# Splitting one group's projection by real and imaginary half instead of by chunk, with the neighbour's half visit moved between the two

## The chip, the cores and the metric

The kernel runs on one core of a Trainium2 chip. The metric is the device time of one execution in microseconds (us). A profiled execution has a "span" as well, from its first to its last recorded instruction; it is some 2 us shorter than the metric. All runs quoted here were timed on the same chip as runs of the kernel before. Times "at" some microsecond are counted from the start of the span.

## The reference, cut to what matters

The output is `x + S5(xn) + MoE(xn)`, where `xn` is the layer norm of `x` (2048 tokens of 1024).

```python
# state-space layer (S5), 1024 complex states
Lam_bar = exp(dt * Lam)
B_bar   = ((Lam_bar - 1) / Lam)[:, None] * (B_re + 1j * B_im)
Bu      = einsum("bld,pd->blp", xn + 0j, B_bar)        # projection into the states
h[t]    = Lam_bar * h[t-1] + Bu[t]                     # recurrence over 2048 tokens
y       = 2 * einsum("blp,dp->bld", h, C).real + xn * Dskip
# mixture of experts: the two tokens with the largest r = xn @ w_r get an MLP on top
...
```

The complex projection is two real ones, with `B_re` and with `B_im`. The change touches only the order in which parts of it are computed at the very start.

## The kernel before

Tokens go in 8 frames of 256 (two chunks of 128 each), states in 8 groups of 128. For a frame `f` and a group `j`, TensorE computes the real and the imaginary half of the projection into one PSUM tile; one such piece of work is called a visit. ScalarE evicts the tile (`evac_u`), VectorE rotates, scans and rotates back, and TensorE multiplies by C.

```python
def stage_Bu(f, j, ts_=slice(0, TF)):              # TF = 256 tokens, T = 128
    if (f, j) not in pB_tiles:
        pB_tiles[f, j] = psum.tile([128, 2, TF], F32, name="pB", tag="B", bufs=3)
    pB = pB_tiles[f, j]
    for ri in range(2):                            # real, imaginary
        for k in range(DT):                        # 8 blocks of the inner dimension
            nc.tensor.matmul(out=pB[:, ri, ts_], lhsT=BT[ri][j][:, k, :], rhs=xnT_tiles[f][:, k, ts_],
                             start=(k == 0), stop=(k == DT - 1))

def evac_u(f, j):
    ...
    nc.scalar.copy(out=u_tiles[f][:, :, j, :], in_=pB_tiles.pop((f, j))[:])

HALVES = ((0, 0), (0, 1), (1, 0), (1, 1), (1, 2))  # these are visited one chunk at a time
```

For the pairs in `HALVES` there are two visits, `("Bh", f, j)` on the first chunk and `("Bu", f, j)` on the second, so that TensorE has work before the second chunk is normalized. Each of them needs the real *and* the imaginary weights of its group. The weights come by transposed loads, real ones first.

The order on every engine is not written down. Each piece of work is a task with a modelled duration, dependencies and a key; a small list scheduler plays the program through and emits the tasks in the order that comes out. `ADJUST` holds hundreds of fitted offsets to the keys.

```python
add(("Bh", f, j), "PE", 0.93, ..., [("B", j, 0), ("B", j, 1), ("xnT", f * CPF)] + ..., key=2 * f - 3 + j / 8, ...)
...
pl.run().emit()
```

## Time and profile before

| | before |
|---|---|
| time, median of the 3 runs made before the prediction (range) | 266.6 us (266.29 to 266.65) |
| span of the profiled execution | 264.4 us |
| TensorE / VectorE / ScalarE busy | 97% / 95% / 60% |
| TensorE's stall for group 1's imaginary weights | 1.13 us, ending at 13.1 |
| VectorE's wait that follows from it | 0.30 us, to 17.48 |

How to read it: two engines are nearly full and feed each other for the whole span. A stall on one is worth something at the end only if the other moves with it, and if nothing takes it back in the next 250 us. The lines behind the last two rows stand in the prediction below.

### The profile page before, as it was taken

To read this page: it belongs to the slowest core of one execution; us is meant where nothing else is said; L and a number is where in the kernel's file an instruction comes from. 1 tells how busy PE (TensorE), PEld (TensorE's weight loads), DVE (VectorE), ACT (ScalarE), POOL (GpSimd) and SP (SyncE) were. 2 spreads that over 40 slices of the span, in tenths; PEclk is the share of its full clock that TensorE was granted. 3 is DMA by queue.
4 is the path that set the end of the run, shared out by engine and by line. 5 is a ranking of instruction groups with operands and counts; after the bars stand their busy time and mean duration, and the time that the engine had idled before them with its cause. 6 is when DMAs were issued, how large, how long until landed. Compare 5 with 4: busy or idle time off the path is not lost.

```text
span 264.4 us, 5522 instructions
## 1 busy us (share of the span) xinstructions
PE 256.5 (97%) x2207; PEld 173.2 (66%) x2227; DVE 251.5 (95%) x334; ACT 158.9 (60%) x281; POOL 83.6 (32%) x126
## 2 busy tenths in 40 slices
PE   7799999999999999999999999999999999999994
PEld 7799988774688457456756586455864776644461
DVE  6999999999999999999999999999998999999992
ACT  3799999959699999996524447034551533145110
POOL 4221303563545440731040217115260409011100
PEclk9999999999999999999999999999999999999999
DMA  8999999998541125416111197588967884770411
GB/s 180 188 175 218 171 235 229 248 271 293 153 137 57 47 60 165 138 40 183 58 62 60 35 360 237 187 266 287 296 235 253 289 272 175 269 288 20 117 46 40
DMA packets 66165, 46.51 MB, mean 176 GB/s; under 512 B 45844, under 2 KB 52122, under 8 KB 66140
## 3 DMA queue, kind: packets, MB, share of 16 engines
q1 hardware_dynamic: 65788, 45.82, 63.4%
q8 instruction: 17, 0.28, 0.5%
q0 software_dynamic: 144, 0.27, 0.3%
q10 hardware_dynamic: 208, 0.07, 0.1%
q14 instruction: 8, 0.07, 0.1%
HBM read 30.94 MB, written 4.20 MB: 133 GB/s over the span
## 4 chain that ended last, share of the span: by engine, by line
PE 61%; DVE 28%; issue 3%; SPq 2%; ACT 2%; DMA 2%; DVEq 0%
PE pB L646 34%; PE pY L849 20%; DVE gf L718 9%; DVE ot L863 3%; PE pG L1048 3%; DVE hT L759 3%; DVE m L760 3%; DVE v L699 2%; DVE v L697 2%; DVE m L698 2%; DMA BT<-in_A_B_im_dram 2%; DVE gb L711 2%; SPq L286 2%; PE pD L1088 1%; PE pY L842 1%
## 5 line engine op out<-in xcount | busy, mean ns | idle before, releaser
L646 PE MATMUL pB<-xnT,BT 128*128 128x256 bf16 (+1 forms) x1104 | 117.5, 265 | 1.1 <-DMA BT<-in_A_B_im_dram 1.1
L849 PE MATMUL pY<-CT,hT 128*128 128x512 bf16 (+1 forms) x508 | 114.8, 372 | 1.7 <-issue 0.5
L646 PEld LDWEIGHTS <-BT 128*128 128x128 bf16 x1104 | 99.7, 98 | 16.2 <-issue 3.2
L849 PEld LDWEIGHTS <-hT 128*128 128x128 bf16 x528 | 49.1, 98 | 52.6 <-issue 3.2
L734 POOL TENSOR_TENSOR cw<-gf,tL 128x16 f32<-128x16 f32 (+1 forms) x38 | 35.0, 924 | 136.1 <-DVE gf L718 135.2
L718 DVE TENSOR_TENSOR_SCAN gf<-R,v 128x1040 f32<-128x1040 f32 (+1 forms) x38 | 69.0, 1851 | 0.2
L652 ACT CAST u<-pB 128x512 bf16<-128x512 f32 x64 | 36.5, 580 | 34.8 <-PE pB L646 34.7
L724 ACT CAST gb<-gf 128x1024 bf16<-128x1024 f32 (+1 forms) x38 | 32.4, 862 | 24.6 <-DVE gf L718 24.5
L810 ACT ACTIVATE xa<-xr,nmr_all,rstd_all 128x1024 f32<-128x1024 bf16 x12 | 14.9, 1239 | 21.9 <-DMA xr<-in_A_x_dram 8.1
L699 DVE TENSOR_TENSOR v<-v,m 128x2048 bf16<-128x2048 bf16 (+2 forms) x22 | 20.6, 938 | 0.8
L761 DVE TENSOR_TENSOR hT<-hT,m 128x2048 bf16<-128x2048 bf16 (+2 forms) x22 | 20.5, 934 | 0.8
L759 DVE TENSOR_TENSOR hT<-gb,E2c 128x2048 bf16<-128x2048 bf16 (+2 forms) x22 | 20.5, 930 | 0.2
L697 DVE TENSOR_TENSOR v<-u,E1c 128x2048 bf16<-128x2048 bf16 (+2 forms) x22 | 20.4, 928 | 0.2
L760 DVE TENSOR_TENSOR m<-gb,E2s 128x2048 bf16<-128x2048 bf16 (+2 forms) x22 | 20.5, 930 | 0.0
L698 DVE TENSOR_TENSOR m<-u,E1s 128x2048 bf16<-128x2048 bf16 (+2 forms) x22 | 20.4, 930 | 0.0
L863 DVE TENSOR_TENSOR ot<-pY,xa 128x512 bf16<-128x512 f32 (+1 forms) x25 | 16.0, 656 | 2.4 <-PE pY L852 1.8
L749 POOL CAST v<-cy 128x16 bf16<-128x16 f32 (+1 forms) x19 | 14.1, 744 | 1.4
L349 ACT ACTIVATE xn<-xt,nmean_all 128x1024 bf16<-128x1024 bf16 x12 | 13.8, 1149 | 0.3
L742 POOL TENSOR_TENSOR cy<-cw 128x16 f32<-128x16 f32 (+1 forms) x19 | 12.8, 674 | 1.5
L343 ACT ACTIVATE xn<-xt 128x1024 bf16<-128x1024 bf16 x12 | 12.6, 1054 | 0.0
L374 ACT ACTIVATE xn<-xt,nmr_all,rstd_all 128x1024 bf16<-128x1024 bf16 x10 | 12.4, 1241 | 0.3
L750 POOL TENSOR_TENSOR v<-cy,v 128x16 bf16<-128x16 f32 (+1 forms) x19 | 11.1, 586 | 1.5
(153 smaller groups left out, 186.6 us busy)
## 6 DMA issues: line engine op xcount, KB each, us to landing
wt<-in_B_w_up_dram SPq DMA_DIRECT2D x14, 512.0 KB, 5.1
wt<-in_B_w_gate_dram SPq DMA_DIRECT2D x14, 512.0 KB, 3.8
wt<-in_B_w_down_dram SPq DMA_DIRECT2D x14, 512.0 KB, 3.9
xt<-in_A_x_dram SPq DMA_DIRECT2D x16, 256.0 KB, 3.1
xr<-in_A_x_dram SPq DMA_DIRECT2D x16, 256.0 KB, 2.5
out_dram<-ot SPq DMA_DIRECT2D x31, 128.0 KB, 2.6
Drow<-in_A_Dskip_dram SPq DMA_DIRECT2D x1, 256.0 KB
xnT<-xn SPq DMA_TRANSPOSE x10, 2.8
```

The costliest lines, as they stand in the source:

```text
L646: nc.tensor.matmul(out=pB[:, ri, ts_], lhsT=BT[ri][j][:, k, :], rhs=xnT_tiles[f][:, k, ts_], start=(k == 0), stop=(k == DT - 1))
L652: nc.scalar.copy(out=u_tiles[f][:, :, j, :], in_=pB_tiles.pop((f, j))[:])
L697: nc.vector.tensor_tensor(out=rot, in0=u, in1=both(E1c, js), op=ALU.mult)
L698: nc.vector.tensor_tensor(out=m[:, :, js, :], in0=u[:, ::-1], in1=E1s[:, :, js, :], op=ALU.mult)
L699: nc.vector.tensor_add(out=rot, in0=rot, in1=m[:, :, js, :])
L718: nc.vector.tensor_tensor_scan(out=flat(gf), data0=flat(R[:, js, :]), data1=flat(v[:, ri, js, :]), initial=0.0, op0=ALU.mult, op1=ALU.add)
L724: nc.scalar.copy(out=gb_tiles[c][:, ri, js, :], in_=gf_tiles[c, js.start, ri][:, :, 2:])
L734: nc.gpsimd.tensor_tensor(out=cw_tiles[c, js.start][:, ri, :, 0:n], in0=g.unsqueeze(1).to_broadcast([128, 2, n]), in1=tL[:, ri, :, js], op ...
L759: nc.vector.tensor_tensor(out=rot, in0=g, in1=E2c[:, :, js, :], op=ALU.mult)
L760: nc.vector.tensor_tensor(out=m[:, :, js, :], in0=g[:, ::-1], in1=both(E2s, js), op=ALU.mult)
L849: nc.tensor.matmul(out=pY[:], lhsT=h_tiles[c][:, ri, j, :], rhs=CT[ri][h][:, j, d0:d0 + w], start=first and c in SKIP_DVE and ri == rs[0] ...
L863: nc.vector.tensor_add(out=y_tiles["ot", c][:, d_], in0=y_tiles.pop(("pY", c, dh))[:], in1=y_tiles["xa", c][:, d_])
```

## The change

Its intent: the first visit of group 1 shall need only the real weights, so that TensorE doesn't stand still until the imaginary ones land. Group 1 of frame 0 is split by half (real over 256 tokens, then imaginary over 256 tokens) in place of by chunk. The first visit of frame 1's group 0 gets an offset of -4.0, which brings it between the two. Cut to its core:

```diff
@@ ADJUST
+    ('Bh', 1, 0): -4.0,
@@
-    def stage_Bu(f, j, ts_=slice(0, TF)):
+    def stage_Bu(f, j, ts_=slice(0, TF), ris=(0, 1)):
...
-        for ri in range(2):
+        for ri in ris:
...
+    RISPLIT = ((0, 1),)
...
-  add(("Bh", f, j), ..., lambda f=f, j=j: stage_Bu(f, j, slice(0, T)), ...
+  add(("Bh", f, j), ..., lambda f=f, j=j: stage_Bu(f, j, ris=(0,)) if (f, j) in RISPLIT else stage_Bu(f, j, slice(0, T)), ...
-  add(("Bu", f, j), ..., lambda ...: stage_Bu(f, j, slice(T if hs else 0, TF)),
+  add(("Bu", f, j), ..., lambda ...: stage_Bu(f, j, ris=(1,)) if (f, j) in RISPLIT else stage_Bu(f, j, slice(T if hs else 0, TF)),
```

On TensorE the four runs of 8 matmuls of 128 columns become two runs of 8 of 256, with frame 1's visit between them.

More of the change, by code (lines that the diff above doesn't have):

```diff
@@ L662 @@
             if hs:
-                add(("Bh", f, j), "PE", 0.93, lambda f=f, j=j: stage_Bu(f, j, slice(0, T)), [("B", j, 0), ("B", j, 1), ("xnT", f * CPF)] + ([] if f else [("xnT0",)]),
+                add(("Bh", f, j), "PE", 0.93, lambda f=f, j=j: stage_Bu(f, j, ris=(0,)) if (f, j) in RISPLIT else stage_Bu(f, j, slice(0, T)), [("B", j, 0), ("B", j, 1), ("xnT", f * CPF)] + ([] if f else [("xnT0",)]),
                     key=2 * f - 3 + j / 8, takes=[("pB", (f, j), [("u", f, j)])])
-            add(("Bu", f, j), "PE", 0.93 if hs else 1.75, lambda f=f, j=j, hs=hs: stage_Bu(f, j, slice(T if hs else 0, TF)),
+            add(("Bu", f, j), "PE", 0.93 if hs else 1.75, lambda f=f, j=j, hs=hs: stage_Bu(f, j, ris=(1,)) if (f, j) in RISPLIT else stage_Bu(f, j, slice(T if hs else 0, TF)),
                 [("B", j, 0), ("B", j, 1)] + [("xnT", f * CPF + cc) for cc in range(CPF)] + ([("Bu", f, j - 1)] if j else [])
```

## The prediction

> **What bounds the kernel now.** I read the page first, then the chain of waits, then the timeline of each engine around the changed stage, then the list of waits of TensorE and VectorE for the whole span.
>
> ```profile
> span 264.4 us, 5522 instructions
> PE 256.5 (97%) x2207; PEld 173.2 (66%) x2227; DVE 251.5 (95%) x334; ACT 158.9 (60%) x281; POOL 83.6 (32%) x126
> ```
>
> Two engines, not one, are nearly full: TensorE 97%, VectorE 95%. A microsecond taken from one of them is worth nothing where the other sets the pace. The chain of waits (start, length, what) begins like this:
>
> ```profile
> 7.65 5.42 DMA BT<-in_A_B_im_dram
> 13.08 0.05 issue
> 13.12 0.62 PE pB L646 x8
> 13.74 0.18 PE r_ps L425 x8
> 13.92 1.81 PE pB L646 x32
> ```
>
> It comes from the transposed load of the imaginary weights of group 1, goes along TensorE to about 56 us, along VectorE from 66 to 119, along TensorE to about 230, and ends on VectorE and TensorE. The load that starts it is the one that this change is aimed at. TensorE's timeline there (start, length, engine, line, operation, tiles, count, idle time before with its releaser):
>
> ```profile
> 9.46 1.05 PE L646 MATMUL pB<-xnT,BT 128*128 128x128 bf16 x16
> 10.35 0.39 PE L430 MATMUL warm<-ident 128*128 128x128 bf16 x4
> 10.93 0.62 PE L403 MATMUL pT<-ident,xn 128*128 128x128 bf16 x8 [0.19 <-DVE xn L363]
> 11.38 0.61 PE L646 MATMUL pB<-xnT,BT 128*128 128x128 bf16 x8
> 13.12 0.62 PE L646 MATMUL pB<-xnT,BT 128*128 128x128 bf16 x8 [1.13 <-DMA BT<-in_A_B_im_dram]
> 13.58 0.34 PE L425 MATMUL r_ps<-wr_cm,xnT 128*128 128x1 bf16 x8
> 13.78 1.95 PE L646 MATMUL pB<-xnT,BT 128*128 128x128 bf16 x32
> 15.57 0.61 PE L403 MATMUL pT<-ident,xn 128*128 128x128 bf16 x8
> ```
>
> At 11.38 the real half of the first chunk of group 1 runs; then TensorE stands still for 1.13 us until the imaginary weights land at 13.08. The 32 matmuls from 13.78 are the second chunk of group 1, then the first visit of frame 1's group 0. It is TensorE's only wait over 0.2 us between 1.4 and 258 us.
>
> ScalarE and VectorE in the same stage:
>
> ```profile
> 14.87 0.58 ACT L652 CAST u<-pB 128x512 bf16<-128x512 f32 x1 [0.55 <-PE pB L646]
> 15.36 1.06 ACT L343 ACTIVATE xn<-xt 128x1024 bf16<-128x1024 bf16 x1
> 16.41 1.05 ACT L545 ACTIVATE sf<-th 128x1024 f32<-128x1024 f32 x1
> 17.48 0.69 DVE L615 CAST E1s<-sf 128x1024 bf16<-128x1024 f32 x1 [0.30 <-ACT sf L545]
> ```
>
> This is how TensorE's stall reaches VectorE: the eviction of group 1 waits 0.55 us, the statistics pass and the sine table queue behind it, and VectorE waits 0.30 us for the sine table. After that VectorE's list of waits has nothing until after 119 us.
>
> **What the Trainium skill says.** "TensorE: Matmul & The Clock Gate", section "Wait — 56ns, not 53.3ns?", gives a warm start-to-start of N / 2.4 GHz plus about 2.5 ns: 55.6 ns for 128 columns, so 109 ns for 256. The trace agrees: (10.35 - 9.46) / 16 = 55.6 ns; and 32 matmuls of 256 columns from 30.07 to the next instruction at 33.57 make 109 ns. The same page's section "Back-to-back issue gap" gives some 81 ns for a weight load with a 128-column matmul in a real kernel; the trace does not agree here, since each of those 16 has its own weight load. This decides whether wider matmuls save time: by the trace hardly any.
>
> "DMA: Bandwidth & Descriptors", section "Anatomy of one DMA — SWDGE (gpsimd) path", puts most of a transfer's fixed cost of about 2 us into the write receipt before its semaphore. Here the issue of the load ended at 9.00 (7.65 + 1.35) and it landed at 13.08, 4.1 us later[...]. The kernel can only work around it, which is what the change does.
>
> The TensorE page's section on the 16 sub-arrays says that ScalarE and VectorE take their queues strictly in order. The three ScalarE lines above agree: the sine table's input is ready before the sine starts, and it starts when the instruction ahead of it ends.
>
> **The change part by part.**
>
> 1. *Matmuls of group 1.* Removed: 4 runs of 8 at 128 columns, 32 x 55.6 ns = 1.78 us. Added: 2 runs of 8 at 256 columns, 16 x 109 ns = 1.75 us. Saving 0.03 us; 16 weight loads fewer, all of them beside matmuls.
>
> 2. *The wait.* The first visit now needs only the real weights, which were there at 11.38, and the second chunk's input, evicted before 9.2. It runs 11.38 to 12.25. Next come the eight 128x1 matmuls and frame 1's moved half visit, both on chunk 2's input; its eviction on ScalarE starts at 11.58 and takes 1.01 us, so it ends at 12.59. Then: 128x1 matmuls 12.64 to 12.84 (0.20, as from 13.58 to 13.78), half visit 16 x 55.6 = 0.89 to 13.73, imaginary visit of group 1 (landed at 13.08, no wait) 0.87 to 14.60. Before, the same work ended at 15.57. TensorE's lead: 0.97 us, made of 1.13 of stall and 0.03 less 0.39 of a new, shorter wait for the eviction, with rounding and hand-overs.
>
> 3. *What that lead is worth.* It is consumed by VectorE:
>
> ```profile
> 36.81 0.54 DVE L358 TENSOR_SCALAR xn<-xt,nmean_all,rstd_all 128x1024 bf16<-128x1024 bf16 x1
> 37.41 0.62 PE L403 MATMUL pT<-ident,xn 128*128 128x128 bf16 x8
> 119.14 0.38 PE L842 MATMUL pY<-dgD,xnT 128*128 128x128 bf16 x4 [0.16 <-DVE ot L863]
> ```
>
> At 37.41 TensorE transposes a normalized chunk that VectorE finished at 37.35: slack 0.06 us. A lead of 0.97 us becomes a wait there unless VectorE is earlier too. The same holds for the first additions into the output at 66.05 (a PSUM ring of three) and at 119.14, where TensorE already waits for VectorE. VectorE has no wait between 17.48 and 119, so it moves only by what the change takes off its 0.30 us.
>
> 4. *VectorE's 0.30 us.* In the same ScalarE order, the eviction of group 1 can start after the imaginary visit ends, 14.60 plus 0.2 of pipeline tail: 14.80 against 14.87, and VectorE gains about 0.07. The half visit was put before the imaginary one, so the group is complete hardly sooner. But instructions are ordered by a list scheduler in the kernel, which thinks the two visits alike in length; there group 1's completion moves one half visit (0.93 in its units) later. ScalarE may then take the statistics pass first, which fits into the 0.55 us of waiting: pass from 14.35, eviction to about 15.95, sine from 15.95 in place of 16.41, and the whole 0.30 goes. I give the first order one chance in three, the second two in three: about 0.2 us.
>
> Sum: 266.6 - 0.2 to 0.3, so 266.3 us.
>
> **The rivals.**
> - *The whole lead arrives*: 266.6 - 1.0 = 265.6. For it: the wait stands on the chain. Against it: the 0.06 us of slack at 37.41 and a VectorE without waits for 100 us.
> - *The next weights become the wait.* TensorE comes to groups 2 to 7 a microsecond sooner. The imaginary load of group 2 was issued at 12.53, that of group 1 took 5.4 us; by that, 17.9, and it would be wanted at 17.1 in place of 18.0. Against it: the earlier transfers queued behind others. It costs only lead that VectorE takes anyway, so 266.5 or so.
> - *The scheduler shuffles later work.* All orders after this point come out of the same simulation; a different tie can move an eviction or an addition by one instruction on VectorE or TensorE (0.7 to 2 us each). The order was tuned for the kernel before, so it is rather worse than better: 266 to 268. For it: hundreds of fitted offsets. Against it: the three visits together take the scheduler's TensorE the same time.
> - *Wider matmuls save weight loads*, as the 81 ns would have it: 32 x 81 against 16 x 109 is 0.85 us. The measured 55.6 ns speaks against it, and item 3 would swallow it.
>
> **Range and chances.** Runs of the kernel before spread over 0.36 us. Between the whole lead with a little more (265.3) and a mild shuffle (267.2) lie most cases. 2% is 5.3 us, five times the stall; only a badly shuffled order could reach it.
>
> **What would show it.** In the changed profile: 8 matmuls of 256 columns at about 11.4 with no wait on the imaginary weights after them; a short wait near 12.6 for the eviction of chunk 2; the 32 matmuls of the stage done near 14.6; the sine table at 16.3 or at 15.9, and VectorE's 0.30 gone in the second case; new TensorE waits on VectorE, 0.6 to 0.9 us in sum, at the transposes near 29 and 37 or near 66. I am wrong if the end moves by over 0.6 us, if TensorE shows no new waits on VectorE, or if VectorE's order differs after 20 us.

## More of the kernel before

The residual input of each chunk is loaded a second time, into a tile with one buffer, and ScalarE consumes it:

```python
xrp = ctx.enter_context(tc.tile_pool(name="xrp", bufs=1))
...
def load_xr(c):
    xr = xrp.tile([128, D], BF16, name="xr")
    nc.sync.dma_start(out=xr[:], in_=x2[c * 128:(c + 1) * 128, :])
```

And `keep_clock` gives TensorE dummy matmuls during the first microseconds, tasks `("warm", i)`.

## The result, and the profile after

| | before | after |
|---|---|---|
| median of 6 runs | 266.59 us | 266.67 us |
| range | 265.90 to 266.65 | 266.38 to 267.21 |
| ratio after / before, 95% interval | | 1.0011 (0.9995 to 1.0027) |

All outputs are right.

The head of the page of the changed kernel:

```profile
span 264.7 us, 5510 instructions
PE 256.9 (97%) x2211; PEld 172.2 (65%) x2211; DVE 251.3 (95%) x334; ACT 159.0 (60%) x281; POOL 83.6 (32%) x126
```

The 16 weight loads are gone (2227 to 2211). Matmuls seem to have grown from 2207 to 2211, but in the trace of before some matmul records are missing. Nothing else has moved, and the span is 0.3 us longer, not shorter. So did the early stage fail to gain? TensorE's timeline there:

```profile
12.16 1.05 PE L647 MATMUL pB<-xnT,BT 128*128 128x256 bf16 x8 [0.54 <-DMA BT<-in_A_B_re_dram]
13.05 0.34 PE L426 MATMUL r_ps<-wr_cm,xnT 128*128 128x1 bf16 x8
13.25 1.93 PE L647 MATMUL pB<-xnT,BT 128*128 128x128 bf16 x24
15.01 0.61 PE L404 MATMUL pT<-ident,xn 128*128 128x128 bf16 x8
```

The wait for the imaginary weights is gone. In its place the real weights came late in this execution: they landed at 12.12, where they had landed at 10.51 before, and cost 0.54 us. Even so the transposes after the stage start at 15.01 in place of 15.57. ScalarE and VectorE:

```profile
14.41 1.06 ACT L344 ACTIVATE xn<-xt 128x1024 bf16<-128x1024 bf16 x1
...
15.47 0.57 ACT L653 CAST u<-pB 128x512 bf16<-128x512 f32 x1
15.96 1.06 ACT L546 ACTIVATE sf<-th 128x1024 f32<-128x1024 f32 x1
...
17.18 0.69 DVE L616 CAST E1s<-sf 128x1024 bf16<-128x1024 f32 x1
```

The statistics pass now fills the time in which ScalarE used to wait 0.55 us for the eviction's input. The sine table starts at 15.96 in place of 16.41, and VectorE's wait of 0.30 us before the cast of that table is gone: 17.18 in place of 17.48. By 20 us VectorE is 0.4 us ahead of the kernel before, and it keeps this lead within 0.02 us until 107 us. So the change does deliver a gain; it is lost later.

Where it is lost is seen when the timelines of the two kernels are laid side by side around 107 us. First the kernel before, one or two rows each from the timelines of SyncE (which issues transfers; start, length of the issue), ScalarE, TensorE and VectorE:

```profile
101.69 1.66 SPq L867 DMA_DIRECT2D out_dram<-ot  x1
103.87 0.34 SPq L805 DMA_DIRECT2D xr<-in_A_x_dram  x1
...
107.10 1.24 ACT L810 ACTIVATE xa<-xr,nmr_all,rstd_all 128x1024 f32<-128x1024 bf16 x1
...
113.20 1.91 PE L646 MATMUL pB<-xnT,BT 128*128 128x256 bf16 x16
...
119.78 1.23 DVE L759 TENSOR_TENSOR hT<-gb,E2c 128x2048 bf16<-128x2048 bf16 x1
```

The same rows of the changed kernel:

```profile
101.29 0.36 SPq L869 DMA_DIRECT2D out_dram<-ot  x1
102.70 0.34 SPq L807 DMA_DIRECT2D xr<-in_A_x_dram  x1
...
107.76 1.24 ACT L812 ACTIVATE xa<-xr,nmr_all,rstd_all 128x1024 f32<-128x1024 bf16 x1 [1.00 <-DMA xr<-in_A_x_dram]
...
113.86 1.91 PE L647 MATMUL pB<-xnT,BT 128*128 128x256 bf16 x16 [0.97 <-ACT u L653]
...
120.44 1.23 DVE L761 TENSOR_TENSOR hT<-gb,E2c 128x2048 bf16<-128x2048 bf16 x1 [1.10 <-ACT gb L726]
```

Read the brackets from top to bottom. ScalarE waits 1.00 us for `xr`, the second load of the residual input. The eviction that follows it in ScalarE's order comes later by that much, so TensorE waits 0.97 us; the copy `gb` of the scan comes later too, so VectorE waits 1.10 us. Before the wait, the changed kernel was 0.4 us ahead, and after it, it is 0.66 us behind (107.76 against 107.10, 113.86 against 113.20, 120.44 against 119.78). VectorE then skips a wait of 0.44 us that the kernel before had at 125 us (0.32 us regained), and the remaining 0.34 us stay to the end.

The strange part is in the first two rows: `xr` was issued 1.17 us *earlier* than before (102.70 against 103.87), and landed later, at 107.68 against 107.02. The transfer's completion comes in 16 parts. Fifteen of them were there at 105.78; the last came 1.9 us after. What ran beside it? The view of the DMA queues shows packets of the kind "instruction", and queue 8 carries large ones. Its row for the stretch 100.5 to 103.5 us of the kernel before (packets, MB, share of 16 engines), and its row for 103.5 to 106.5 us of the changed one; each kernel has no such packet in the other stretch:

```profile
q8 instruction: 1, 0.02, 3.4%
```

```profile
q8 instruction: 1, 0.02, 2.7%
```

Over the whole span this queue has 17 packets and 0.28 MB in both kernels, 16 KB each. The Trainium skill, page "Runtime: NRT & Kernel Launch", section "Instruction fetch mechanics", says that an engine's instructions are refilled in blocks of 16 KiB, 256 instructions, over a DMA queue of the sequencer's own, and that this is mostly hidden. The count fits TensorE alone: its 2211 matmuls and 2211 weight loads make 4422 / 256 = 17.3, and on the page no other engine has more than 334 instructions. That queue 8 is TensorE's is inferred from this; the trace doesn't name its owner. A share of 2.7% of 16 engines for 3 us is 0.027 x 16 x 3 = 1.3 us of one DMA engine. In the kernel before, this fetch started at 101.57, while SyncE was issuing the output store (whose issue took 1.66 us in place of 0.36), and so it was over before `xr` was issued. In the changed kernel it started at 104.79, in the middle of `xr`'s transfer, and ended at 106.06.

What `xr`'s last part did after that can be read from the packets. The load is 256 KB in 16 parts, so 16 KB or 8 packets of 2 KB each. One line of the DMA view of the changed kernel, for 106.04 to 107.20 us:

```profile
DMA packets 218, 0.07 MB, mean 61 GB/s; under 512 B 209, under 2 KB 210, under 8 KB 218
```

Exactly 8 packets of 2 KB or more are left, one part's worth. In the packed trace they run one after another from 106.05 to 107.19: they start when the fetch ends. In the kernel before, `xr` already had nothing to spare: it landed at 107.02 and was used at 107.10, and these 0.08 us are the hand-over, which takes 0.08 to 0.09 us in every trace here in which ScalarE waits for `xr`.

This gives the theory: **32 fewer instructions on TensorE move its instruction fetches, one of them now falls into a transfer that has no slack, and this takes back the gain.** Rivals: the lead itself makes the wait (everything comes 0.4 us earlier, `xr`'s issue among it); the new order on TensorE makes it; chance does.

### The profile page after: what moved, and what is told of

The parts are those of the page before. It is cut to its first block, busy times and chain, and to the rows that moved or that the text cites. A ratio compares the mean times of both kernels' runs of the same rounds, so it can differ in the third digit from the quotient of the medians.

```text
span 264.7 us, 5510 instructions
## 1 busy us (share of the span) xinstructions
PE 256.9 (97%) x2211; PEld 172.2 (65%) x2211; DVE 251.3 (95%) x334; ACT 159.0 (60%) x281; POOL 83.6 (32%) x126
## 4 chain that ended last, share of the span: by engine, by line
PE 62%; DVE 18%; ACT 11%; DMA 5%; issue 3%; SPq 0%; ACTq 0%
PE pY L851 29%; PE pB L647 26%; DVE gf L720 3%; PE pG L1050 3%; DMA wt<-in_B_w_down_dram 2%; ACT xn L350 2%; DMA xr<-in_A_x_dram 2%; ACT xa L812 2%; ACT xn L344 2%; DVE st L335 2%; ACT xn L375 1%; ACT gb L726 1%; PE pY L844 1%; PE pD L1090 1%; DVE ot L865 1%
## 5 line engine op out<-in xcount | busy, mean ns | idle before, releaser
L851 PE MATMUL pY<-CT,hT 128*128 128x512 bf16 (+1 forms) x528 | 118.3, 373 | 0.0
L751 POOL CAST v<-cy 128x16 bf16<-128x16 f32 (+1 forms) x19 | 14.1, 744 | 1.4
```

Of the source, the lines that this page charges most:

```text
L851: nc.tensor.matmul(out=pY[:], lhsT=h_tiles[c][:, ri, j, :], rhs=CT[ri][h][:, j, d0:d0 + w], start=first and c in SKIP_DVE and ri == rs[0] ...
```

## The experiments

Ten runs were made, of nine kernels (`e0_after` is the changed kernel, `e10_swap_again` repeats `e4_swap_only`). Two ideas were given up. With a second buffer for `xr`, 14.1 KB per partition are left for the pool of the expert weights, which needs 16 KB. A dependency that forces the eviction ahead of the statistics pass deadlocked the list scheduler, so in the kernels below two tasks are exchanged after scheduling instead.

### The changed kernel again: `e0_after`

No edit; it tells chance from cause.

> The changed kernel once more, as the comparison for the others. Theory (instruction fetch): VectorE is 0.3 to 0.4 us ahead of the kernel before from 17 to 107 us, then ScalarE waits about 1 us for the load of xr at about 107, since a 16 KB instruction fetch of TensorE at 104 to 105 us holds one DMA engine; time 266.5 to 266.8, ratio to before 1.000 to 1.002. Rival (chance): the wait at 107 was an accident of the one profiled run and is not there again; then 266.2.

Measured: 266.53 us (265.77 to 267.51), ratio 0.9997 (0.9973 to 1.0022). The wait came again; the fetch started at 104.77, and `xr`'s last part came 2.3 us after its fifteenth:

```profile
107.84 1.25 ACT L812 ACTIVATE xa<-xr,nmr_all,rstd_all 128x1024 f32<-128x1024 bf16 x1 [1.11 <-DMA xr<-in_A_x_dram]
```

In this execution the real weights were in time, so it is the better one to test the early steps of the prediction. Three rows of TensorE's timeline, and one of its list of waits (total, times, longest):

```profile
11.42 1.04 PE L647 MATMUL pB<-xnT,BT 128*128 128x256 bf16 x8
12.69 0.35 PE L426 MATMUL r_ps<-wr_cm,xnT 128*128 128x1 bf16 x8 [0.23 <-ACT xnT L416]
...
14.67 0.61 PE L404 MATMUL pT<-ident,xn 128*128 128x128 bf16 x8
```

```profile
PE pT L404 <- DVE xn L359: 0.4, 1, 0.4
```

The visit starts at 11.42 without a wait, a short wait for the eviction of chunk 2 follows, and the stage ends 0.90 us earlier than before. At the transpose near 37 us TensorE then waits 0.4 us for VectorE. VectorE's own lead at 100 us is 0.45 us, half of TensorE's.

### The same order with the instructions put back: `e1_halves`

```diff
         for ri in ris:
-            for k in range(DT):
-                nc.tensor.matmul(out=pB[:, ri, ts_], ..., rhs=xnT_tiles[f][:, k, ts_], ...)
+            for t_ in ((slice(0, T), slice(T, TF)) if len(ris) == 1 else (ts_,)):
+                for k in range(DT):
+                    nc.tensor.matmul(out=pB[:, ri, t_], ..., rhs=xnT_tiles[f][:, k, t_], ...)
```

Order and intent are those of the change; only the two visits of group 1 are cut into 128 columns again, so TensorE has as many instructions as before.

> The changed kernel with each of the two visits by real and imaginary half run as two runs of 128 columns, so that TensorE has as many instructions as before (the change took 32 out) and its 16 KB instruction fetches fall where they fell before; the order of work on every engine is that of the changed kernel. Theory (instruction fetch): the fetch near 104.8 us goes back to about 101, no wait of ScalarE for xr at 107, VectorE's lead of 0.3 to 0.4 us reaches the end: span 264.0, time 266.2, ratio to before 0.9985. Rival (TensorE's lead itself shifts the transfers against each other): the wait at 107 stays, time as the changed kernel's. Rival (width): 32 narrow matmuls cost more than 16 wide ones, by under 0.05 us, not to be seen.

Measured: 266.36 us (265.76 to 267.21), ratio 0.9991 (0.9971 to 1.0011). The fetch is back at 101.38, and of the wait 0.23 us are left:

```profile
107.10 1.24 ACT L813 ACTIVATE xa<-xr,nmr_all,rstd_all 128x1024 f32<-128x1024 bf16 x1 [0.23 <-DMA xr<-in_A_x_dram]
```

VectorE was 0.31 us ahead at 100 us and still 0.32 us at 250 us, and the span is 264.0. The rival "new order on TensorE" falls with this. The small remaining wait comes of the lead and of the fetch's length together: the fetch lasted 1.67 us, `xr` was issued only after it, at 103.95, and landed at 107.02 as in the kernel before, and ScalarE wanted it 0.3 us sooner. The lead alone does not make even this wait, as the next run has a larger lead and none.

### Only the half visit moved: `e3_move_only`

The kernel before plus the one line in `ADJUST`; no split.

> The kernel before with the half visit of frame 1's group 0 moved, without the split into real and imaginary. TensorE keeps its stall of about 1.1 us on the imaginary weights; ScalarE takes the statistics pass first, as in the changed kernel. The group's eviction can start at about 15.8 in place of 14.9, so the sine table comes at 16.3 in place of 16.4: VectorE gains 0.1 us. Instruction fetches as before. Theory: span 264.3, time 266.5, ratio 0.9995. Rival (the stall's removal is what counts): 266.6, no change at all, and VectorE's 0.30 stays.

Measured: 266.13 us (265.72 to 267.38), ratio 0.9990 (0.9969 to 1.0011). The expectation of the early stage was missed: in this execution the imaginary weights happened to land in time, so there was no stall to keep. VectorE was 0.47 us ahead at 100 us and 0.48 us ahead at 250 us; the fetch was at 101.11, and `xr` caused no wait. In this execution a lead as large as that of the changed kernel thus passes 107 us unharmed, with no instruction missing. The experiment said nothing about what the move by itself is worth.

### Only ScalarE's order exchanged: `e4_swap_only`, and again: `e10_swap_again`

The kernel before, with the exchange that the scheduler had made as a by-product:

```diff
-    pl.run().emit()
+    pl.run()
+    pl.order.remove(("u", 0, 1))
+    pl.order.insert(pl.order.index(("sum", 4)) + 1, ("u", 0, 1))
+    pl.emit()
```

> The kernel before with nothing but ScalarE's two instructions exchanged, the statistics pass ahead of the eviction of group 1: TensorE's program is untouched and keeps its stall of 1.1 us. Theory (only VectorE's 0.30 us counts): sine table at 16.0 in place of 16.4, VectorE's wait of 0.30 gone, a lead of 0.3 us to the end: span 264.1, time 266.3, ratio 0.999. Rival (TensorE's stall is what the time rests on): no gain, ratio 1.000 and VectorE waits again later for TensorE.

Measured: 266.18 us (265.92 to 266.30) against 266.62 us of the kernel before, ratio 0.9981 (0.9965 to 0.9996). Two rows of ScalarE's timeline:

```profile
15.94 1.06 ACT L545 ACTIVATE sf<-th 128x1024 f32<-128x1024 f32 x1
...
106.64 1.23 ACT L810 ACTIVATE xa<-xr,nmr_all,rstd_all 128x1024 f32<-128x1024 bf16 x1
```

The sine table is as early as in the changed kernel (15.94 against 15.96), although the imaginary weights still cost TensorE 0.56 us in this execution. VectorE's lead is 0.44 us, and in this execution there is no wait at 107 us. So VectorE's gain in the change can be had whole from the exchange on ScalarE.

> The exchange of ScalarE's two instructions in the kernel before, once more, to see whether its gain is repeated in other rounds. Theory (only VectorE's 0.30 us counts, fetches as before): ratio 0.998 to 0.999, span 263.9 to 264.1, no wait of ScalarE for xr near 107. Rival (the first result was luck of the rounds): ratio 1.000 with the lead of VectorE still there at 100 us but not at the end.

Measured on the repeat: 266.13 us (265.81 to 267.09), ratio 0.9998 (0.9981 to 1.0014). Its profile has the wait at 107 us with 0.40 us, though the fetch was at 101.30; VectorE's lead fell from 0.33 to 0.18 us after it. The fetch lasted 1.76 us here, against 1.19 us in the first run, and `xr` was issued at 103.96 in place of 103.23. The gain of 0.2% was resolved once and not confirmed. If it is there, it is near 0.1%, the limit of what these runs resolve.

### Only the split: `e2_split_only`

The changed kernel without the line in `ADJUST`.

> The changed kernel without the moved half visit: the split alone. ScalarE's order is that of the kernel before (eviction of group 1 first), TensorE has 32 instructions fewer than before. The imaginary visit ends near 14.0, so the eviction waits for nothing, the sine table comes at about 15.95 and VectorE's 0.30 us is gone here too: the move isn't needed for the gain. Theory (instruction fetch): fetch at 104 to 105 us, ScalarE waits about 1 us for xr near 107, span 264.7, time 266.5 to 266.8. Rival: no wait at 107 and span 264.0, if the loss needs the moved visit.

Measured: 266.23 us (266.08 to 266.80), ratio 0.9997 (0.9978 to 1.0017). The eviction starts at 14.32 without a wait and the sine table at 15.87, so VectorE's 0.30 us is gone here too, with ScalarE's order unchanged: the exchange is one road to the gain, and this is a second. VectorE is 0.48 us ahead at 100 us; the fetch is at 104.51, the wait at 107 us is 1.10 us, and VectorE is 0.38 us behind at 250 us. The half visit plays no part in the loss; the split with its 32 instructions does.

### The changed kernel with the old order on ScalarE: `e5_evict_first`

```diff
-    pl.run().emit()
+    pl.run()
+    pl.order.remove(("sum", 4))
+    pl.order.insert(pl.order.index(("u", 0, 1)) + 1, ("sum", 4))
+    pl.emit()
```

> The changed kernel with ScalarE's exchange undone: eviction of group 1 ahead of the statistics pass. Theory (the 0.30 us comes through ScalarE's order, not through TensorE's saved stall): sine table at 16.3, VectorE waits 0.2 to 0.3 us for it again, lead of VectorE under 0.15 us at 100 us, the wait for xr at 107 stays, so span 264.9 to 265.1, time 266.9. Rival (the exchange is of no account): span 264.7 and VectorE's wait gone as in the changed kernel.

Measured: 267.60 us (267.13 to 267.95), ratio 1.0044 (1.0024 to 1.0064), slower than expected, and all six runs of it. The real weights were late (0.5 us) in the profiled execution, and now ScalarE has nothing to do meanwhile:

```profile
15.42 0.59 ACT L653 CAST u<-pB 128x512 bf16<-128x512 f32 x1 [0.80 <-PE pB L647]
```

VectorE waits 0.55 us for the sine table, more than the 0.30 us of before, and is 0.53 us behind at 100 us; 0.30 us of that it had lost before 8 us, ahead of any work on group 1. The wait at 107 us (fetch at 105.91, 1.15 us) comes on top. The expectation had this wait and not the larger loss before it. With the half visit between its two halves, the split is thus no gain for VectorE unless ScalarE's order changes: group 1 is complete no sooner, and with the statistics pass behind it the eviction is exposed to whatever the weights do. Why all six executions are slow is not shown, as one of them was profiled.

### Half the instructions taken out: `e7_half_pad`

As `e1_halves`, but only the imaginary visit is cut into 128 columns (`if ris == (1,)`), so 16 instructions fewer than before.

> The changed kernel with only the imaginary visit in runs of 128 columns: TensorE has 16 instructions fewer than before, in place of 32. Theory (instruction fetch): the fetch comes between that of before (101.6) and that of the changed kernel (104.8), near 103; xr is then held on one engine for part of the time: ScalarE's wait at 107 between 0.3 and 1.0 us, span 264.0 to 264.5. Rival (chance): no wait, or the full one, whatever the fetch.

Measured: 266.21 us (265.79 to 267.46), ratio 1.0002 (0.9978 to 1.0026). The fetch started at 103.90, between the two other places, and lasted 0.99 us; `xr` landed at 106.50, with no wait. A part of the wait was expected, and none came. The start of the fetch does follow the count; whether it hurts depends on when it ends. It ended at 104.89, and `xr`'s last part landed 1.61 us later, still in time for its use at 106.72.

### The instructions taken out elsewhere: `e8_swap_fewer_warm`

This is the strongest control. It is `e4_swap_only`, with no split and no moved visit, and 32 instructions fewer in the dummy work at the start:

```diff
-    def keep_clock():
-        for _ in range(2):
+    def keep_clock(n):
+        for _ in range(n):
...
-        add(("warm", i), ..., keep_clock, ...
+        add(("warm", i), ..., lambda i=i: keep_clock(1 if 4 <= i < 20 else 2), ...
```

> ScalarE's exchange alone, as in the run that held 263.9, and 16 warm-up matmuls with their weight loads taken out of TensorE's first five microseconds, where TensorE waits for data anyway: 32 instructions fewer, as in the changed kernel, but nothing else of the change. Theory (instruction fetch): the fetch moves from 101 to 104 or 105 us, ScalarE waits about 1 us for xr near 107, span 264.7, time 266.6 to 266.8, although no work was added. The first fetch moves as well, from 9.7 to 11 us, so the stall on the imaginary weights of group 1 is gone or elsewhere. Rival (the loss comes from the split or the moved visit): span stays at 263.9, time 266.2.

Measured: 267.27 us (266.38 to 268.28), ratio 1.0032 (1.0006 to 1.0057). The wait is there, with the fetch at 104.90:

```profile
108.80 1.24 ACT L810 ACTIVATE xa<-xr,nmr_all,rstd_all 128x1024 f32<-128x1024 bf16 x1 [1.11 <-DMA xr<-in_A_x_dram]
```

VectorE falls from 0.51 us behind at 100 us to 1.38 us behind at 250 us. The first fetch did move, to 11.79 us, and TensorE had no stall for group 1's weights. The 0.51 us before the wait were not expected. TensorE ran slower at first:

```profile
8.07 1.74 PE L646 MATMUL pB<-xnT,BT 128*128 128x128 bf16 x16
```

These 16 matmuls take 1.53 us from their start to that of the next work, 96 ns each in place of 55.6. TensorE's granted clock was 0.62 of full speed from 8 to 9 us, 0.50 from 9 to 11 us and 0.67 from 11 to 12 us in this execution, against 1.00 in that of `e4_swap_only`. Three of the six executions have a mean clock of 0.991 or 0.992; no execution of another kernel is under 0.996. That the missing dummy work brings this is likely, but only this run has it. So this run is a worse kernel for two reasons, of which only the second bears on the theory. It bears on it well: these 32 instructions are not those of the change, VectorE has no lead here, and the microsecond is lost at the same place.

### The split by halves without the move, instructions kept: `e9_split_halves`

`e1_halves` without the line in `ADJUST`; a candidate for a version that beats both.

> The split by real and imaginary half in runs of 128 columns, without the moved half visit: TensorE has as many instructions as before, ScalarE's order is that of before, and the group is complete sooner because the imaginary visit comes straight after the real one. Theory: VectorE's 0.30 us gone by the other road (eviction near 14.4, sine near 15.95), fetch near 101, no wait or one under 0.3 us for xr near 107, span 263.9 to 264.1, ratio 0.998 to 0.999. Rival (the split itself costs something later): span 264.5 or more with TensorE's fetch at 101.

Measured: 265.91 us (265.81 to 266.56) against 266.35 us of before in that call, ratio 0.9990 (0.9977 to 1.0004). Fetch at 101.21, no wait at 107 us, VectorE 0.37 us ahead at 100 us and 0.38 us at 250 us, span 264.0. It has the best median of all, and is still not resolved from the kernel before.

### All profiled executions side by side

"Instructions" is TensorE's count against before. The two landing times are those of the fifteenth and the last part of `xr`. VectorE's column is its position against before at 100 and at 250 us (minus is ahead). All in us.

| kernel | instructions | fetch: start (length) | `xr` 15th / last | ScalarE's wait | VectorE 100 / 250 | span |
|---|---|---|---|---|---|---|
| before | 0 | 101.57 (1.63) | 106.78 / 107.02 | 0 | 0 / 0 | 264.4 |
| after | -32 | 104.79 (1.27) | 105.78 / 107.68 | 1.00 | -0.41 / +0.35 | 264.7 |
| `e0_after` | -32 | 104.77 (1.38) | 105.49 / 107.75 | 1.11 | -0.45 / +0.41 | 264.8 |
| `e2_split_only` | -32 | 104.51 (1.60) | 106.12 / 107.72 | 1.10 | -0.48 / +0.38 | 264.8 |
| `e5_evict_first` | -32 | 105.91 (1.26) | 106.68 / 108.77 | 1.15 | +0.53 / +1.44 | 265.8 |
| `e8_swap_fewer_warm` | -32 | 104.90 (2.19) | 106.70 / 108.72 | 1.11 | +0.51 / +1.38 | 265.7 |
| `e7_half_pad` | -16 | 103.90 (0.99) | 105.82 / 106.50 | 0 | -0.36 / -0.20 | 264.2 |
| `e1_halves` | 0 | 101.38 (1.67) | 106.86 / 107.02 | 0.23 | -0.31 / -0.32 | 264.0 |
| `e3_move_only` | 0 | 101.11 (0.92) | 105.89 / 105.93 | 0 | -0.47 / -0.48 | 263.9 |
| `e4_swap_only` | 0 | 101.14 (1.19) | 106.01 / 106.40 | 0 | -0.44 / -0.45 | 263.9 |
| `e10_swap_again` | 0 | 101.30 (1.76) | 107.09 / 107.16 | 0.40 | -0.33 / -0.18 | 264.2 |
| `e9_split_halves` | 0 | 101.21 (1.39) | 106.04 / 106.30 | 0 | -0.37 / -0.38 | 264.0 |

In all five profiles with 32 instructions fewer, the last part of `xr` is 1.6 to 2.3 us behind its fifteenth, and ScalarE waits 1.0 to 1.15 us. In the seven others the gap is under 0.7 us and the wait 0.40 us at most. What goes with the wait is the count, and not the split (absent in `e8_swap_fewer_warm`), the moved visit (absent in `e2_split_only`), or a lead (absent in `e5_evict_first` and `e8_swap_fewer_warm`).

The link between fetch and wait is closer than the count. In all six profiles with instructions missing, the fetch falls into `xr`'s transfer, and its last part lands 1.60 to 1.62 us after the fetch's end, though the fetch lasts from 0.99 to 2.19 us. In the five with 32 fewer, exactly 8 packets of 2 KB remain after the fetch, and the first starts within 0.02 us of its end. So the last sixteenth of `xr` is held up until the fetch is over. In the six profiles with the count kept, the fetch falls on the issue of the output store instead: that issue takes 1.18 to 2.06 us in place of 0.36, and `xr` is issued 0.67 to 0.90 us after the fetch's end. There a long fetch makes `xr` late too (0.23 us of wait in `e1_halves`, 0.40 us in `e10_swap_again`), only less.

All this rests on the profiles. The times do not resolve a loss of a few tenths of a microsecond: the kernels with the wait and VectorE's lead have ratios of 1.0011, 0.9997 and 0.9997 to the kernel before, and `e1_halves` was timed at 266.36 us beside 266.53 us of `e0_after`, with ranges that overlap.

Two things stay open. First, the fetch moved by 3.2 us for 32 instructions, while 16 matmuls of 256 columns with their weight loads, as TensorE runs them there, take an estimated 16 x 109 ns = 1.75 us; what triggers a fetch beyond the count is not known. Second, the spans of the changed kernel's timed executions are 264.7, 265.3, 264.0, 264.6, 265.4 and 264.0, and those of its repeat 264.8, 264.0, 264.1, 263.9, 264.9 and 265.1. Five of these twelve are as short as those of kernels without the wait. It may be that they escape it, but no execution without a profile shows its instructions, and both profiled ones had it.

## Why the prediction was right or wrong

The number was right: 266.3 was predicted with 265.3 to 267.2 as the range, and 266.67 came out. But the road to it was wrong in one step, and the number was right partly by luck: the expected gain was small, and the range reached from 1.3 us of gain to a loss of 0.6 us.

- **Item 1, wider matmuls save nothing.** Right: the eight of 256 columns take 0.89 us to the next work (12.16 to 13.05). The rival with 81 ns per pair falls. What the item missed is that 16 weight loads and 16 matmuls fewer are not free of effect when they are free of time.
- **Item 2, TensorE's lead of 0.97 us.** Right in mechanism, including the new short wait for chunk 2's eviction. In `e0_after` the size is right too, 0.90 us. (The terms listed beside the 0.97 us make only 0.77: the stall of 1.13 us is counted from the modelled end of the last matmul. From the time that its 8 starts took, 11.38 + 0.45 = 11.83, to 13.12 it is 1.29 us, and so 0.93 us come out.) In the profile after it was 0.56 us, since the real weights landed late. The prediction took the landing times of one trace for fixed. In executions of programs that are the same up to that point, the waits for group 1's weights came out at 1.13 us (before), 0.56 (`e4_swap_only`), 0.20 and 0.41 (`e10_swap_again`) and 0 (`e3_move_only`). In the kernel before, the first packet of queue 8 starts near 9.7 us, and DMA traffic falls to 6 GB/s from 11 to 12 us. In the six profiles with such a wait, the imaginary weights land 1.7 to 1.8 us after that packet's end, and their load was issued at 7.58 us or later; in five of the six without, it was issued at 7.39 or earlier (the sixth is `e8_swap_fewer_warm`, whose packet comes at 11.79). So a late issue that meets the fetch goes with the stall; no run here separates the two.
- **Item 3, VectorE takes most of the lead.** Right: at the transposes near 37 us TensorE was held to VectorE's pace. The "0.6 to 0.9 us" of new waits were too much: 0.4 us in `e0_after` and 0.13 us in the profile after, whose lead was smaller and of which VectorE had kept more.
- **Item 4, VectorE's 0.30 us.** The second order, to which two chances in three were given, is the one that came, with the sine table at 15.96 where 15.95 was written. VectorE gained somewhat more than its wait of 0.30 us: the cast starts 0.61 us after the start of the copy before it, in place of 0.98 us. Its lead was 0.4 us although its first load had come 0.09 us later.
- **The sum, "266.6 - 0.2 to 0.3".** This is the step that failed. It lets VectorE's lead run to the end because nothing in VectorE's list of waits stood in its way, "has nothing until after 119 us". The lead did run on to 107 us, and there met a load without slack. With the fetch in the middle of the load, ScalarE waited 1.00 us for it, and 0.41 us ahead became 0.35 us behind. Where the count was kept (`e1_halves`, `e9_split_halves`), the lead did reach the end, and the spans are 0.3 to 0.4 us shorter than before, as item 4 and the sum have it.
- **The rivals.** The scheduler's shuffle was confined to one exchange, and that one was the useful one. The whole lead didn't arrive. That the next weights would become the wait was near the mark in kind, a load, but at the wrong place: it was the weights of the same group, and by chance.
- **What the prediction looked at too little:** the slack of transfers whose consumer doesn't wait. A wait of zero in the list looks the same whether the load landed long before its use or, as `xr` here, 0.08 us before it.

## What to carry to other kernels

When a change makes one engine earlier, look beyond the waits that exist: list the loads that land just in time for their use, for these turn into waits first, and follow the lead through the later trace until the end. Count the instructions that a change removes from an engine that has thousands of them, as they move its later instruction fetches (here by 2.9 to 4.3 us near 101 us), and a fetch can fall into a transfer. Putting the count back, or taking as many out elsewhere, is a cheap test of that, and the packets of the late transfer show whether they start when the fetch ends. And before calling a stall at the start of a kernel a fixed cost, look at several executions of it.

## What the Trainium skill lacked or had wrong

- "Runtime: NRT & Kernel Launch", "Instruction fetch mechanics": the blocks of 16 KiB agree (17 packets, 0.28 MB). It says that crossing a block is mostly hidden. No run here contradicts this for the engine that fetches, but the page lacks what it does to others: each of the packets listed above took 0.9 to 2.2 us, and where one fell into a 256 KB load, the load's last sixteenth started only when it had ended and landed 1.60 to 1.62 us after that; where one fell on the issue of a store, that issue took 1.18 to 2.06 us in place of 0.36.
- No page that I read says that removing instructions moves later fetches: 32 fewer on TensorE moved the fetch near 101 us by 2.9 to 4.3 us, 16 fewer by 2.3 us.
- "TensorE: Matmul & The Clock Gate", "Back-to-back issue gap": 81 ns for a weight load with a matmul of 128 columns in a real kernel. Here it is 55.6 ns (16 pairs from 9.46 to 10.35 us), the figure that the page gives for a matmul alone.
- No page that I read says how much the landing of the same load varies between executions: here the real weights of group 1 landed at 10.51 us in one and at 12.12 us in another, with the same program up to that point.
